# Horner's form for the numerator of a rational function: ScalarE makes one straight line in place of two, VectorE makes the rest

## The chip, the cores and the metric

The program runs on one core of a Trainium2 chip. The metric is the device time of one execution in microseconds (us); a median over several runs is given. The engines are named as in the profile: PE (TensorE, matmuls), PEld (its weight loads), DVE (VectorE), ACT (ScalarE), POOL (GpSimd) and SP (SyncE, which issues DMAs). SBUF is the on-chip memory of 128 partitions, PSUM the accumulator memory of 8 banks that PE writes.

## The reference

Two attentions (one over tokens averaged in fours, one over a band of 7 neighbours) are added, and the sum x of 4608 tokens by 512 goes through a two-layer network whose activation is a rational function:

```python
h = x @ w_in                                   # 4608 x 2048
h2 = h * h
h3 = h2 * h
P = a[0] + a[1] * h + a[2] * h2 + a[3] * h3
Q = 1.0 + np.abs(b[0]) * np.abs(h) + np.abs(b[1]) * h2
g = P / (Q + 1e-06)
return (g @ w_out).astype(np.float32)          # 4608 x 512
```

All is float32. The products with w_in and w_out are made with each operand split into a high and a low part, and three of the four part products are kept.

## The kernel before

The tokens are cut into ten blocks, eight of 512 tokens and two of 256 that collect remainders. A block of 512 tokens has 16 steps, one for each 128 columns of w_in; a block of 256 has 8 steps of 256 columns. That makes 144 steps, n = 0 to 143, and each handles a tile of 128 x 512 values of h.

A step has three parts. h_part makes h in one PSUM bank: 12 matmuls of 128x512 (L733), or in the first 16 steps 4 matmuls on unsplit operands (L721). The banks alternate: step n+2 writes the bank of step n, so it must wait until everything that reads h of step n has read it. middle (L748) turns h into g, as a high part gh and a low part gl. o_part, two steps later, multiplies gh and gl with the split w_out in 12 matmuls (L798) into four other banks that hold the block's output.

In middle, ScalarE reads h from PSUM four times: Abs with scale b0 into tb, Square into tq, and two straight lines, ta = a3*h + a2 and u = a1*h + a0 (all L746). VectorE then works on SBUF alone: tb = b1*tq + tb (L761), ta = ta*tq (L766), ta = ta + u (L767). ScalarE makes tq = exp(-ln(tb + 1.000001)), which is 1/Q, in two operations (Ln, Exp). VectorE makes gh = ta*tq (L770) and the low part by three more operations (L773, L778, L779). The tile u lies in the same memory as gh, and log (the result of Ln) in that of gl, so both can be written only when the o_part of step n-2 has read gh and gl.

The attention for a later block runs in between, in groups of two head pairs, called quads here. A quad is, for each pair: scores on PE (L417, L427), a maximum on DVE (L459, L466), exponentials on ACT (L474); pooled scores on PE (L444), their maximum on DVE (L489, L494), exponentials on ACT (L500); normalisation on DVE and ACT (L511, L512, L535, L517); transposes on PE (L548, L555) and copies of them on ACT (L561, L571, L572); and two groups of matmuls with v (L594, L582). The attention uses the PSUM banks 0 and 1. Two quads serve a block. The quads of the first block run ahead of step 0, those of the second in the first 16 steps, and twelve more between step 16 and step 112. In the first 16 steps the weights are also prepared (L338 to L361 on ACT and DVE).

The order on each engine is fixed before the program runs. A planner takes every piece of work with a cost in us, an engine and the tiles that it reads and writes, and places the pieces in a list (Plan.run); the engines then take their instructions strictly in that order. The planner knows of writes before reads and reads before writes. It holds no rule on two engines that read one tile. The framework under it adds the semaphore waits.

Of the kernel before, what the change touches and what calls it, by code (L numbers as in the profile page):

```python
# [13 lines left out]
AF = mybir.ActivationFunctionType  # L14
ALU = mybir.AluOpType
# [61 lines left out]
class Plan:  # L77
# [11 lines left out]
    def add(self, engine, dur, fn, reads=(), writes=(), due=None, lag=None):  # L89
        t = Task()  # L90
        t.engine, t.dur, t.fn, t.due, t.n = engine, dur, fn, due, len(self.tasks)
        t.lag, t.preds, t.succs, t.late, t.start = lag, {}, [], 1e9, None
        rk = set().union(*(r.keys for r in reads)) if reads else set()
        wk = set().union(*(w.keys for w in writes)) if writes else set()
        for k in rk | wk:
            w = self.writer.get(k)
            if w is not None:
                t.preds[w] = True
        for k in wk:
            for r in self.readers.get(k, ()):  # L100
                t.preds.setdefault(r, False)
            self.writer[k] = t
            self.readers[k] = []
        for k in rk - wk:
            self.readers[k].append(t) if k in self.readers else self.readers.__setitem__(k, [t])
        t.preds.pop(t, None)
        for p in t.preds:
            p.succs.append(t)
        self.tasks.append(t)
        return t  # L110
# [75 lines left out]
def attention_moe(  # L186
# [13 lines left out]
    scale = 1.0 / 8.0  # L200
    nc.scalar.preload_act_table_set("natural_log_exp_and_others")
    plan = Plan()
    add = plan.add
# [5 lines left out]
    def put(name, shape, dtype, at=None):  # L209
        nonlocal top  # L210
        offset = top if at is None else at
        n = 2 if dtype == BF16 else 4
        for d in shape[1:]:
            n *= d
        if at is None:
            top = -(-(offset + n) // 32) * 32
        ap = nc.alloc_sbuf_tensor_at(name, shape, dtype, offset=offset).ap()
        room = Room(ap, (("S", k) for k in range(offset // 32, -(-(offset + n) // 32))))
        room.at = offset
        room.size = n  # L220
        return room
# [26 lines left out]
    gb = [put(f"gb{i}", [P, DM], F32, g.at) for i, g in enumerate(gt)]  # L248
# [3 lines left out]
    cf = put("cf", [P, 8], F32)  # L252
# [47 lines left out]
    a0, a1, a2, a3 = (cf.ap[:, i : i + 1] for i in range(4))  # L300
# [405 lines left out]
    def bank_h(n):  # L706
        return banks[HFIRST[n]] if n < len(HFIRST) else hb[n % 2]
# [37 lines left out]
    def act(cost, out_, room_in, in_, func, *more, **kw):  # L745
        add("ACT", cost, lambda: nc.scalar.activation(out=out_.ap, in_=in_, func=func, **kw), (room_in, cf, *more), (out_,))  # L746

    def middle(n):  # L748

        ta, tb, tq = (mt[2 * i + n % 2] for i in range(3))  # L750
        gh, gl = gt[n % 2], gt[2 + n % 2]
        u, log = gb[n % 2], gb[2 + n % 2]
        h = bank_h(n)
        act(0.58, tb, h, h.ap, AF.Abs, scale=b0)
        act(0.48, tq, h, h.ap, AF.Square)
        act(0.66, ta, h, h.ap, AF.Identity, scale=a3, bias=a2)
        act(0.66, u, h, h.ap, AF.Identity, scale=a1, bias=a0)
        v = nc.vector
        add(
            "DVE", 0.66,  # L760
            lambda: v.scalar_tensor_tensor(  # L761
                out=tb.ap, in0=tq.ap, scalar=b1, in1=tb.ap, op0=ALU.mult, op1=ALU.add
            ),
            (tq, tb, cf), (tb,),
        )
        add("DVE", 0.61, lambda: v.tensor_tensor(out=ta.ap, in0=ta.ap, in1=tq.ap, op=ALU.mult), (ta, tq), (ta,))  # L766
        add("DVE", 0.61, lambda: v.tensor_tensor(out=ta.ap, in0=ta.ap, in1=u.ap, op=ALU.add), (ta, u), (ta,))  # L767
        act(0.63, log, tb, tb.ap, AF.Ln, bias=cone)
        act(0.54, tq, log, log.ap, AF.Exp, scale=-1.0)
        add("DVE", 0.61, lambda: v.tensor_tensor(out=gh.ap, in0=ta.ap, in1=tq.ap, op=ALU.mult), (ta, tq), (gh,))  # L770
        add(
            "DVE", 0.61,
            lambda: v.scalar_tensor_tensor(  # L773
                out=tb.ap, in0=tb.ap, scalar=CONE, in1=gh.ap.bitcast(F32), op0=ALU.add, op1=ALU.mult
            ),
            (tb, gh), (tb,),
        )
        add("DVE", 0.61, lambda: v.tensor_tensor(out=tb.ap, in0=ta.ap, in1=tb.ap, op=ALU.subtract), (ta, tb), (tb,))  # L778
        add("DVE", 0.61, lambda: v.tensor_tensor(out=gl.ap, in0=tb.ap, in1=tq.ap, op=ALU.mult), (tb, tq), (gl,))  # L779

    def o_part(n, f):
# [123 lines left out]
    for n in range(NS + LAG):  # L905
        if n < NS:
            k, s = steps[n]
            for f in range(blocks[k].fg):
                h_part(n, f)
                if n < NAT:  # L910
                    parts(0, n, due_h(n + blocks[0].nstep) - 2.0)
                    if n == NAT - 1 and NAT < blocks[0].nstep:
                        split_x(0, due_h(NAT) - 3.0)
            if s == blocks[k].nstep - 1:

                if k + 1 < len(blocks):
                    split_x(k + 1)
        o = n - LAG
        if o >= 0:
            k, s = steps[o]  # L920
            for f in range(blocks[k].fg):
                o_part(o, f)
            if s == blocks[k].nstep - 1:
                store(k)

                if blocks[k].b is None and blocks[k - 1].b + 2 < B:
                    attend(blocks[k - 1].b + 2)
                elif blocks[k].b is not None and blocks[k].b + 2 < B and blocks[k + 1].b is not None:
                    attend(blocks[k].b + 2)
        if n < NS:  # L930
            middle(n)
# [10 lines left out]
    for t in pe:  # L942
        n = int(WARM * (t.start - end) / 0.107)
# [91 lines left out]
```

## Time and profile before

| | us |
|---|---|
| median of 3 runs | 974.91 (974.35 to 976.29) |
| the profiled execution | 975.71 |
| its span in the trace | 973.9 |

The span is the time from the first to the last instruction of the program in the trace; the 1.8 us beside it lie around the span. The granted TensorE clock was 0.997 over the run.

The profile's page gives the busy time of each engine, a chain of work that ended last (followed back from the end, at each step to what released an instruction), and groups of instructions by line with their mean duration. Durations overlap a little: an engine starts its next instruction before the one ahead is quite finished, so the distance from start to start is shorter than the duration. A duration counts where another engine waits for the result, the distance where the engine itself is full.

| engine | busy, us | share of the span |
|---|---|---|
| PE | 959.7 | 99% |
| DVE | 838.4 | 86% |
| ACT | 810.5 | 83% |
| POOL | 147.1 | 15% |

### The profile page before, as it was taken

To read this page: it belongs to the slowest core of one execution; us is meant where nothing else is said; L and a number is where in the kernel's file an instruction comes from. 1 tells how busy PE (TensorE), PEld (TensorE's weight loads), DVE (VectorE), ACT (ScalarE), POOL (GpSimd) and SP (SyncE) were. 2 spreads that over 40 slices of the span, in tenths; PEclk is the share of its full clock that TensorE was granted. 3 is DMA by queue.
4 is the path that set the end of the run, shared out by engine and by line. 5 is a ranking of instruction groups with operands and counts; after the bars stand their busy time and mean duration, and the time that the engine had idled before them with its cause. 6 is when DMAs were issued, how large, how long until landed. Compare 5 with 4: busy or idle time off the path is not lost.

```text
span 973.9 us, 19825 instructions
## 1 busy us (share of the span) xinstructions
PE 959.7 (99%) x7383; PEld 759.8 (78%) x7383; DVE 838.4 (86%) x1474; ACT 810.5 (83%) x2076; POOL 147.1 (15%) x176
## 2 busy tenths in 40 slices
PE   7999999999999999999999999999999999999997
PEld 5665657887887879988878888878788787998885
DVE  6899999998888888888789887888788888888886
ACT  6899998978789887689787979798888988867774
POOL 1221322120302121002221121203030210000000
PEclk9999999999999999999999999999999999999999
DMA  9984654332424342023333333324243320100001
GB/s 318 297 264 126 160 126 114 76 69 69 83 94 65 87 73 73 1 60 68 76 76 94 85 66 86 85 85 86 66 83 100 56 46 2 44 1 23 1 1 43
DMA packets 46359, 83.43 MB, mean 86 GB/s; under 512 B 6552, under 2 KB 29080, under 8 KB 46264
## 3 DMA queue, kind: packets, MB, share of 16 engines
q1 hardware_dynamic: 25912, 63.00, 19.4%
q0 software_dynamic: 20352, 19.19, 14.3%
q8 instruction: 58, 0.95, 0.4%
q14 instruction: 37, 0.30, 0.1%
HBM read 72.72 MB, written 9.44 MB: 84 GB/s over the span
## 4 chain that ended last, share of the span: by engine, by line
PE 92%; ACT 5%; DVE 2%; issue 1%; DMA 0%; DVEq 0%; ACTq 0%
PE psum L798 40%; PE psum L733 37%; PE psum L721 4%; PE psum L582 3%; PE psum L594 2%; PE psum L548 2%; PE psum L555 2%; PE psum L427 2%; ACT el L474 2%; PE psum L444 1%; ACT m L746 1%; PE psum L417 1%; ACT ep L500 1%; PE psum L937 0%; ACT gb L746 0%
## 5 line engine op out<-in xcount | busy, mean ns | idle before, releaser
L798 PE MATMUL psum<-wh,g 128*128 128x512 f32 x1152 | 371.6, 404 | 0.9 <-DVE g L779 0.9
L733 PE MATMUL psum<-xs,wh 128*128 128x512 f32 (+1 forms) x1152 | 267.4, 369 | 0.0
L746 ACT ACTIVATE m<-psum,cf 128x512 f32<-128x512 f32 x288 | 215.9, 753 | 42.8 <-PE psum L733 40.6
L798 PEld LDWEIGHTS psum<-wh,g 128*128 128x128 f32 x1152 | 209.0, 189 | 49.4 <-issue 4.3
L733 PEld LDWEIGHTS psum<-xs,wh 128*128 128x128 f32 x1152 | 200.3, 189 | 36.9 <-ACT gb L746 0.3
L798 PE MATMUL psum<-wl,g 128*128 128x512 f32 x576 | 225.3, 392 | 0.0
L746 ACT ACTIVATE gb<-psum,cf 128x512 f32<-128x512 f32 x144 | 115.9, 805 | 48.4 <-PE psum L798 48.2
L394 POOL DMA_DIRECT2D pq<-in_qkp_dram x84 | 73.8, 908 | 468.5 <-DMA pq<-in_qkp_dram 384.1
L733 PE MATMUL psum<-xs,wl 128*128 128x512 f32 (+1 forms) x576 | 143.3, 371 | 0.0
L770 DVE TENSOR_TENSOR g<-m,m 128x512 fp32r<-128x512 f32 x144 | 99.2, 689 | 33.7 <-ACT m L746 31.6
L798 PEld LDWEIGHTS psum<-wl,g 128*128 128x128 f32 x576 | 108.6, 189 | 23.7
L767 DVE TENSOR_TENSOR m<-m,gb 128x512 f32<-128x512 f32 x144 | 99.2, 689 | 27.0 <-ACT gb L746 24.3
L761 DVE SCALAR_TENSOR_TENSOR m<-m,cf,m 128x512 f32<-128x512 f32 x144 | 107.4, 745 | 12.1 <-ACT m L746 11.9
L474 ACT ACTIVATE el<-psum,nm 128x64 f32<-128x64 f32 x320 | 97.5, 356 | 23.8 <-DVE nm L466 23.8
L733 PEld LDWEIGHTS psum<-xs,wl 128*128 128x128 f32 x576 | 100.0, 189 | 17.6 <-issue 1.0
L746 ACT ACTIVATE gb<-m,cf 128x512 f32<-128x512 f32 x144 | 107.2, 744 | 2.1 <-DVE m L761 2.1
L766 DVE TENSOR_TENSOR m<-m,m 128x512 f32<-128x512 f32 x144 | 98.5, 684 | 5.6 <-ACT m L746 5.6
L773 DVE SCALAR_TENSOR_TENSOR m<-m,g 128x512 f32<-128x512 f32 x144 | 99.4, 691 | 3.2
L778 DVE TENSOR_TENSOR m<-m,m 128x512 f32<-128x512 f32 x144 | 99.3, 690 | 2.7
L779 DVE TENSOR_TENSOR g<-m,m 128x512 fp32r<-128x512 f32 x144 | 98.2, 682 | 1.2
L746 ACT ACTIVATE m<-gb 128x512 f32<-128x512 f32 x144 | 93.3, 648 | 4.9 <-DVE m L766 2.1
L394 POOL DMA_DIRECT2D vp<-in_vp_dram x84 | 71.2, 880 | 164.1 <-DMA vp<-in_vp_dram 155.9
(64 smaller groups left out, 989.0 us busy)
## 6 DMA issues: line engine op xcount, KB each, us to landing
qk<-in_qk_dram SPq DMA_DIRECT2D x32, 590.0 KB
pq<-in_qkp_dram POOLq DMA_DIRECT2D x84, 144.0 KB, 3.3
vw<-in_vw_dram SPq DMA_DIRECT2D x32, 320.0 KB
out_dram<-xf SPq DMA_DIRECT2D x32, 256.0 KB
vp<-in_vp_dram POOLq DMA_DIRECT2D x84, 72.0 KB, 2.8
sx<-in_w_in_dram SPq DMA_DIRECT2D x11, 512.0 KB
sx<-in_w_out_dram SPq DMA_DIRECT2D x11, 512.0 KB
pq<-in_qkp_dram SPq DMA_DIRECT2D x28, 144.0 KB
```

Source lines behind the costliest of these rows:

```text
L394: lambda d=dst, x=src, r=r: nc.gpsimd.dma_start(out=d.ap, in_=x[b, r, :, i], accum_op=ALU.add),
L474: nc.scalar.activation(out=s.el.ap[:, k, c.pos(j), :], in_=view[:, j, k, :], func=AF.Exp, bias=nm[:, 5 * j + k : 5 * j + k + 1], scale=sca ...
L733: nc.tensor.matmul(ph.ap[:, f * t : (f + 1) * t], lhsT=(high, low)[j][0][fc].ap[:, c, :], rhs=blk.x[i].ap[:, c, :], start=(part_ == 0 and ...
L746: add("ACT", cost, lambda: nc.scalar.activation(out=out_.ap, in_=in_, func=func, **kw), (room_in, cf, *more), (out_,))
L761: lambda: v.scalar_tensor_tensor(out=tb.ap, in0=tq.ap, scalar=b1, in1=tb.ap, op0=ALU.mult, op1=ALU.add),
L766: add("DVE", 0.61, lambda: v.tensor_tensor(out=ta.ap, in0=ta.ap, in1=tq.ap, op=ALU.mult), (ta, tq), (ta,))
L767: add("DVE", 0.61, lambda: v.tensor_tensor(out=ta.ap, in0=ta.ap, in1=u.ap, op=ALU.add), (ta, u), (ta,))
L770: add("DVE", 0.61, lambda: v.tensor_tensor(out=gh.ap, in0=ta.ap, in1=tq.ap, op=ALU.mult), (ta, tq), (gh,))
L773: lambda: v.scalar_tensor_tensor(out=tb.ap, in0=tb.ap, scalar=CONE, in1=gh.ap.bitcast(F32), op0=ALU.add, op1=ALU.mult),
L778: add("DVE", 0.61, lambda: v.tensor_tensor(out=tb.ap, in0=ta.ap, in1=tb.ap, op=ALU.subtract), (ta, tb), (tb,))
L779: add("DVE", 0.61, lambda: v.tensor_tensor(out=gl.ap, in0=tb.ap, in1=tq.ap, op=ALU.mult), (tb, tq), (gl,))
L798: nc.tensor.matmul(ob[sub].ap, lhsT=g[i].ap[:, f0 : f0 + P], rhs=flat((high, low)[j][1][fc].ap), start=(fc == 0 and m == 0), stop=(fc == N ...
```

## The change

The numerator is computed in Horner's form without its constant: ta = a3*h + a2 on ScalarE as before, then ta = ta*h and ta = (ta + a1)*h on VectorE. The constant a0 is added inside the two later operations that use ta. The tile u and its ScalarE operation are gone. VectorE still has seven operations in a step. Two of them now read h from PSUM (L765 and L768 of the changed kernel), and three that took two tiles, or a tile and a constant of the instruction, take a constant per partition from cf as well.

```diff
-        u, log = gb[n % 2], gb[2 + n % 2]
+        log = gb[2 + n % 2]
...
         act(0.66, ta, h, h.ap, AF.Identity, scale=a3, bias=a2)
-        act(0.66, u, h, h.ap, AF.Identity, scale=a1, bias=a0)
...
-        add("DVE", 0.61, lambda: v.tensor_tensor(out=ta.ap, in0=ta.ap, in1=tq.ap, op=ALU.mult), (ta, tq), (ta,))
-        add("DVE", 0.61, lambda: v.tensor_tensor(out=ta.ap, in0=ta.ap, in1=u.ap, op=ALU.add), (ta, u), (ta,))
+        add("DVE", 0.66, lambda: v.tensor_tensor(out=ta.ap, in0=ta.ap, in1=h.ap, op=ALU.mult), (ta, h), (ta,))
+        add(
+            "DVE", 0.69,
+            lambda: v.scalar_tensor_tensor(out=ta.ap, in0=ta.ap, scalar=a1, in1=h.ap, op0=ALU.add, op1=ALU.mult),
+            (ta, h, cf), (ta,),
+        )
         act(0.63, log, tb, tb.ap, AF.Ln, bias=cone)
         act(0.54, tq, log, log.ap, AF.Exp, scale=-1.0)
-        add("DVE", 0.61, lambda: v.tensor_tensor(out=gh.ap, in0=ta.ap, in1=tq.ap, op=ALU.mult), (ta, tq), (gh,))
+        add(
+            "DVE", 0.66,
+            lambda: v.scalar_tensor_tensor(out=gh.ap, in0=ta.ap, scalar=a0, in1=tq.ap, op0=ALU.add, op1=ALU.mult),
+            (ta, tq, cf), (gh,),
+        )
...
-        add("DVE", 0.61, lambda: v.tensor_tensor(out=tb.ap, in0=ta.ap, in1=tb.ap, op=ALU.subtract), (ta, tb), (tb,))
+        add(
+            "DVE", 0.66,
+            lambda: v.scalar_tensor_tensor(out=tb.ap, in0=ta.ap, scalar=a0, in1=tb.ap, op0=ALU.add, op1=ALU.subtract),
+            (ta, tb, cf), (tb,),
+        )
```

The line numbers of the changed kernel are 12 higher after this place, up to 8 in the middle of it: L761, L766, L767, L770, L773, L778, L779, L798 of before are L760, L765, L768, L776, L781, L788, L791, L810 now; lines up to L746 keep their numbers.

The planner works from the changed list, so the order moves on every engine, and the framework's waits with it. The rows below are those of the built programs; "waits" names the engines (or DMA queues) whose semaphores an instruction waits for itself, and x4 four equal instructions.

**ACT in the quad at steps 99 and 100** (m0, m2, m4 are ta, tb, tq of an even step, m1, m3, m5 those of an odd one; el and ep belong to attention). Before, from the Square of step 99 on:

```order
L746 ACTIVATE m5_169<-psum 128x512
L746 ACTIVATE m1_165<-psum,cf_181 128x512
L474 ACTIVATE el1_203,sm1_188<-psum,nm1_184 128x64 [waits DVE_49,PE_49]
L474 ACTIVATE el1_203,sm1_188<-psum,nm1_184 128x64 x4
L746 ACTIVATE gb1_175<-psum,cf_181 128x512 [waits PE_49]
L474 ACTIVATE el1_203,sm1_188<-psum,nm1_184 128x64 x5
L746 ACTIVATE gb3_177<-m3_167,cf_181 128x512 [waits DVE_49]
L746 ACTIVATE m2_166<-psum,cf_181 128x512 [waits DVE_49,PE_49]
L746 ACTIVATE m5_169<-gb3_177 128x512 [waits Activation_49]
L746 ACTIVATE m4_168<-psum 128x512
L746 ACTIVATE m0_164<-psum,cf_181 128x512
L500 ACTIVATE ep0_199,sm0_187<-psum,nm0_183 128x144 [waits DVE_49,PE_49]
```

With the change, from the line ta of step 99 on:

```order
L746 ACTIVATE m1_165<-psum,cf_181 128x512 [waits PE_49]
L746 ACTIVATE m3_167<-psum,cf_181 128x512
L746 ACTIVATE m5_169<-psum 128x512 [waits DVE_49]
L474 ACTIVATE el1_203,sm1_188<-psum,nm1_184 128x64 [waits DVE_49,PE_49]
L474 ACTIVATE el1_203,sm1_188<-psum,nm1_184 128x64 x4
L746 ACTIVATE gb3_177<-m3_167,cf_181 128x512 [waits DVE_49,PE_49]
L474 ACTIVATE el1_203,sm1_188<-psum,nm1_184 128x64 x5
L746 ACTIVATE m5_169<-gb3_177 128x512 [waits Activation_49]
L746 ACTIVATE m0_164<-psum,cf_181 128x512 [waits PE_49]
L746 ACTIVATE m2_166<-psum,cf_181 128x512 [waits DVE_49]
L746 ACTIVATE m4_168<-psum 128x512 [waits DVE_49]
L500 ACTIVATE ep0_199,sm0_187<-psum,nm0_183 128x144 [waits DVE_49,PE_49]
```

The line ta now stands ahead of Abs and Square in a step, u is gone, and Square waits for DVE. Before, no Square of the 144 steps waited for DVE; now 73 do.

**DVE at the same place.** Before, from the last operation of step 98:

```order
L779 TENSOR_TENSOR g2_172<-m2_166,m4_168 128x512 [waits DVE_49]
L767 TENSOR_TENSOR m1_165<-m1_165,gb1_175 128x512 [waits DVE_49,Activation_49]
L489 TENSOR_REDUCE nm0_183<-psum 128x3 [waits PE_49]
L489 TENSOR_REDUCE nm1_184<-psum 128x3 [waits PE_49,Activation_49]
L494 TENSOR_TENSOR nm0_183<-nm0_183,scales_182 128x3 [waits DVE_49]
L494 TENSOR_TENSOR nm1_184<-nm1_184,scales_182 128x3 [waits DVE_49]
L770 TENSOR_TENSOR g1_171<-m1_165,m5_169 128x512 [waits Activation_49]
L761 SCALAR_TENSOR_TENSOR m2_166<-m4_168,cf_181,m2_166 128x512 [waits Activation_49]
L773 SCALAR_TENSOR_TENSOR m3_167<-m3_167,g1_171 128x512 [waits DVE_49]
L511 TENSOR_SCALAR sm0_187<-sm0_187 128x13 [waits Activation_49]
```

With the change, from the same operation:

```order
L791 TENSOR_TENSOR g2_172<-m2_166,m4_168 128x512 [waits DVE_49]
L768 SCALAR_TENSOR_TENSOR m1_165<-m1_165,cf_181,psum 128x512
L776 SCALAR_TENSOR_TENSOR g1_171<-m1_165,cf_181,m5_169 128x512 [waits DVE_49,PE_49,Activation_49]
L765 TENSOR_TENSOR m0_164<-m0_164,psum 128x512 [waits PE_49,Activation_49]
L489 TENSOR_REDUCE nm0_183<-psum 128x3 [waits PE_49]
L489 TENSOR_REDUCE nm1_184<-psum 128x3 [waits PE_49]
L494 TENSOR_TENSOR nm0_183<-nm0_183,scales_182 128x3 [waits DVE_49]
L494 TENSOR_TENSOR nm1_184<-nm1_184,scales_182 128x3 [waits DVE_49]
L781 SCALAR_TENSOR_TENSOR m3_167<-m3_167,g1_171 128x512
L760 SCALAR_TENSOR_TENSOR m2_166<-m4_168,cf_181,m2_166 128x512 [waits Activation_49]
```

gh of step 99 and L765 of step 100 now stand ahead of the pooled maxima. In the built program the count for which L765 of step 100 waits is that of Abs of the same step, the latest reader of its bank on ACT in the list, and not that of the line ta, whose result it uses; the Square behind waits for that L765. The accesses of ACT and DVE to one bank thus take turns, in the order of the list. The sequence in a step is ta, Abs, L765, Square, L768 in 63 of the 144 steps; ta, Abs, Square, L765, L768 in 32; ta, L765, L768, Abs, Square in 22; Abs, Square, ta, L765, L768 in 14; other mixtures in 13.

**PE behind the pooled scores of the same quad** (wh0 and wl0 are parts of w_in, wh1 and wl1 of w_out; g0 and g2 belong to step 98, g1 and g3 to step 99). Before, from the last o_part of step 98 on:

```order
L798 MATMUL psum<-wl1_10_140,g0_170 128x512
L733 MATMUL psum<-xs1_1_157,wh0_13_69 128x512 x4
L733 MATMUL psum<-xs1_0_156,wl0_13_114 128x512 x4
L733 MATMUL psum<-xs1_0_156,wh0_14_70 128x512 [waits Activation_49]
L733 MATMUL psum<-xs1_0_156,wh0_14_70 128x512 x3
L548 MATMUL psum<-ident_178,ep0_199 72x112 [waits Activation_49] x3
L548 MATMUL psum<-ident_178,ep0_199 72x112 [waits DVE_49]
L548 MATMUL psum<-ident_178,ep0_199 72x112 x2
L798 MATMUL psum<-wh1_11_83,g1_171 128x512 [waits DVE_49]
L798 MATMUL psum<-wh1_11_83,g3_173 128x512 [waits DVE_49]
```

With the change:

```order
L810 MATMUL psum<-wl1_10_140,g0_170 128x512
L733 MATMUL psum<-xs1_0_156,wh0_13_69 128x512 [waits DVE_49]
L733 MATMUL psum<-xs1_0_156,wh0_13_69 128x512 x3
L733 MATMUL psum<-xs1_1_157,wh0_13_69 128x512 x4
L733 MATMUL psum<-xs1_0_156,wl0_13_114 128x512 x4
L810 MATMUL psum<-wh1_11_83,g1_171 128x512 [waits DVE_49]
L810 MATMUL psum<-wh1_11_83,g3_173 128x512 [waits DVE_49]
```

The o_part of step 99 (wh1_11) comes straight behind h of step 101 (wh0_13); before, four matmuls of step 102 (wh0_14) and six transposes stood ahead of it. The first matmul into a bank waits for DVE where it waited for ACT. From step 24 on the list of PE switches to attention 110 times, where it did so 120 times.

## The prediction

> **What bounds the kernel now.** I read the page's busy times and chain first, then the chain in two stretches, then the windows.
>
> ```profile
> PE 959.7 (99%) x7383; PEld 759.8 (78%) x7383; DVE 838.4 (86%) x1474; ACT 810.5 (83%) x2076; POOL 147.1 (15%) x176
> PE 92%; ACT 5%; DVE 2%; issue 1%; DMA 0%; DVEq 0%; ACTq 0%
> by line: PE psum L798 43.1%; PE psum L733 43.0%; PE psum L582 2.8%; PE psum L427 2.2%; PE psum L548 2.2%; PE psum L594 2.2%; PE psum L555 2.1%; PE psum L444 1.7%; PE psum L417 1.0%
> ```
>
> The third line is the chain between 618 and 723 us, a whole block with its two quads: PE alone. Nothing that ACT or DVE gives up there shortens the run; only a new wait of PE counts. The chain leaves PE at the start, in one stretch of the first block, and at the end.
>
> ```profile
> 112.86 1.84 ACT m L746 x3
> ...
> 126.79 0.42 DVE wb L341
> ...
> 153.59 1.39 PE psum L582 x64
> 154.97 4.53 PE psum L798 x12
> 44.00:154.00 110.00, 107.71 (x720) 66.24 (x717) 107.80 (x205) 106.82 (x277) 24.24 (x29) 1.00 0.61 162
> 900.00:930.00 30.00, 30.00 (x134) 24.87 (x133) 25.95 (x40) 21.24 (x34) 0.00 (x0) 1.00 0.00 1
> 690.00:713.00 23.00, 23.00 (x171) 18.48 (x170) 17.40 (x34) 22.81 (x82) 4.38 (x5) 1.00 0.34 76
> ```
>
> The first four rows are pieces of the chain (start, length): from 112.86 to 153.59 us it alternates between ACT and DVE. The other three are windows (length, then busy PE, PEld, DVE, ACT, POOL, clock, DMA). From 44 to 154 us all three engines are nearly full. In a stretch without attention (900 to 930) DVE and ACT have room. In a quad (690 to 713) ACT is full, 22.81 of 23, and DVE idles because it waits for ACT and PE.
>
> **The change part by part.**
>
> ```profile
> L746 ACT ACTIVATE gb<-psum,cf 128x512 f32<-128x512 f32 x144 | 115.9, 805 | 48.4 <-PE psum L798 48.2
> L761 DVE SCALAR_TENSOR_TENSOR m<-m,cf,m 128x512 f32<-128x512 f32 x144 | 107.4, 745 | 12.1 <-ACT m L746 11.9
> L767 DVE TENSOR_TENSOR m<-m,gb 128x512 f32<-128x512 f32 x144 | 99.2, 689 | 27.0 <-ACT gb L746 24.3
> L773 DVE SCALAR_TENSOR_TENSOR m<-m,g 128x512 f32<-128x512 f32 x144 | 99.4, 691 | 3.2
> L535 DVE TENSOR_TENSOR el<-el,sm 128x640 f32<-128x640 f32 x32 | 26.2, 818 | 0.1
> L623 DVE TENSOR_TENSOR xf<-psum,up 128x464 f32<-128x464 f32 x32 | 19.2, 636 | 5.5 <-PE psum L582 5.3
> ```
>
> Removed: u, 144 x 0.805 = 115.9 us of ACT, and 48.2 us in which ACT stood at u until the o_part had read gh. Behind PE's chain this is worth nothing by itself. Log, in the memory of gl, still waits for that o_part.
>
> DVE keeps seven operations. Three become of the kind of L761 (745 ns, a constant per partition from cf) where they were of that of L767 (689 ns); an immediate constant costs nothing more (L773, 691). That is 3 x 0.056 = 0.17 us a step, 24 us in all. Reading PSUM has no price here: from 512 elements (L767) to 640 (L535) is 129 ns, 1.0 ns an element, so 464 elements would take 641 ns from SBUF, and L623 takes 636 with one input in PSUM. I take 0 for it. [...]
>
> In stretches without attention, 25.95 of 30 us of DVE grow by 0.9: 5.5 steps (30 over 2.72 + 2.74, the 12 matmuls of h and of o_part in rows below) x 0.17. PE hides that.
>
> *The turns at the bank.* This decides. Before, ACT alone read h. Now DVE reads it too, and the list of waits shows that L765 waits for Abs or Square, and Square or Abs for L765 or L768. The planner did not place its pieces for that. I walk the quad of steps 97 to 102 with starts and distances of the trace.
>
> ```profile
> 690.70 2.72 PE psum L733 x12
> 697.24 3.64 PE psum L733 x16
> 700.87 0.90 PE psum L444 x24
> 701.77 2.94 PE psum L798 x12
> 693.50 0.78 ACT L746 ACTIVATE gb<-m,cf 128x512 f32<-128x512 f32 x1
> 696.71 0.31 ACT L474 ACTIVATE el<-psum,nm 128x64 f32<-128x64 f32 x1 [0.18 <-DVE nm L466]
> 700.28 0.77 ACT L746 ACTIVATE gb<-m,cf 128x512 f32<-128x512 f32 x1
> 700.89 0.74 ACT L746 ACTIVATE m<-psum,cf 128x512 f32<-128x512 f32 x1
> 701.46 0.69 ACT L746 ACTIVATE m<-gb 128x512 f32<-128x512 f32 x1
> 702.46 0.85 ACT L746 ACTIVATE m<-psum,cf 128x512 f32<-128x512 f32 x1
> 703.12 0.45 ACT L500 ACTIVATE ep<-psum,nm 128x144 f32<-128x144 f32 x1
> 695.11 0.82 DVE L459 TENSOR_REDUCE nm<-psum 128x10 f32<-128x640 f32 x1 [2.20 <-PE psum L427]
> 701.80 1.12 DVE L489 TENSOR_REDUCE nm<-psum 128x3 f32<-128x432 f32 x2 [1.47 <-PE psum L444]
> 703.64 0.75 DVE L761 SCALAR_TENSOR_TENSOR m<-m,cf,m 128x512 f32<-128x512 f32 x1
> 704.30 0.69 DVE L773 SCALAR_TENSOR_TENSOR m<-m,g 128x512 f32<-128x512 f32 x1
> 706.79 0.63 DVE L779 TENSOR_TENSOR g<-m,m 128x512 fp32r<-128x512 f32 x1
> ```
>
> Distances: 0.66 us for L761's kind on DVE, 0.60 for the others; on ACT 0.61 (Ln), 0.57 (Abs), 0.5 (Exp), 0.66 (a line). A waiting engine starts some 0.07 us after the end of what it waits for.
>
> First turn. h of step 99 ends at 690.70 + 2.72 = 693.42. ACT ends the exponentials at 693.44 (0.06 sooner than Ln's 693.50, for Ln takes u's place among them), then Exp, the line ta of step 99 at 693.96, Abs at 694.62, which ends at 695.36. L765 of step 99 waits for that Abs: 695.43. The maximum L459 stands behind it and starts at 696.03 instead of 695.11, and so do the exponentials, 0.92 late: 697.63. Second turn. Two batches of them (1.46 and 1.44), Ln (0.61) and Exp (0.52) bring the line ta of step 100 to 701.66 and Abs to 702.32, end 703.06. L765 of step 100 waits for it, 703.13, and the pooled maxima L489 stand behind that: 703.73 instead of 701.80, 1.93 late. Behind them come their scaling, to 704.97, then L781, L760, L788, a small one and L791, which makes gl of step 99: 0.60 + 0.66 + 0.66 + 0.12 puts its start at 707.01 and its end 0.68 later at 707.69 (706.79 was the start before).
>
> PE without a wait: h of step 100 ends at 697.24 + 2.72 = 699.96; six matmuls of o_part (1.37), the pooled scores (0.90), six more (1.37), 12 of h (2.73) make 706.33. There the o_part of step 99 needs that gl, at about 707.75. PE stands for **1.4 us**. Before, four matmuls and six transposes lay there. Without the turns the same walk has L765 half a us sooner twice, and PE would wait 0.4. ACT and DVE stay late by as much for the rest of the quad, so I do not count it twice or take it back.
>
> The other kind of quad, around step 92, has L765 and L768 both ahead of Abs. There ACT had a gap, which takes up part:
>
> ```profile
> 640.87 0.31 ACT L474 ACTIVATE el<-psum,nm 128x64 f32<-128x64 f32 x1 [1.55 <-DVE nm L466]
> ```
>
> Its price lies between 0 and the 1.4 of the first kind; I take 0.8. Twelve quads lie behind step 16, six of each kind: 6 x 1.4 + 6 x 0.8 = **+13.2 us**. The ends are 0 (all hidden, below) and 12 x 1.4 = 16.8. [...]
>
> *First block.* DVE's idle time from 44 to 154 us is 110 - 107.80 = 2.2; 15 steps add 15 x 0.17 = 2.5 us. ACT loses 15 x 0.8 = 12 us there. DVE full, the stretch grows by 0.3 at least, and by 2.5 if the idle time stays. I take **+1.4**. Below nothing: rival two.
>
> *Switches of PE.* Twelve matmuls of L798 next to attention took 2.94 (above, 701.77), alone 2.74 (below). Ten switches fewer at 0.1 to 0.2: **-1.3**.
>
> *The end.*
>
> ```profile
> 959.69 2.74 PE psum L798 x12
> 962.45 1.40 ACT gb L746 x2
> 963.87 0.64 ACT m L746
> 964.53 0.70 DVE g L770
> 967.55 0.71 PE psum L798 x2
> ```
>
> At 962.45 u waits for the o_part of step 141, and Ln runs behind it. Now Ln starts there, 0.68 sooner, and gives 0.06 back in each of two VectorE operations: **-0.55**.
>
> Sum: 13.2 + 1.4 - 1.3 - 0.55 = +12.75 us. The profiled execution took 975.71, its span 973.9, so 988.5 by it. The median of the runs is 0.8 lower: **987.6 us**, 1.3% slower.
>
> **The rivals.**
>
> One, the turns are hidden. For it speaks that ACT has 4 x 0.8 = 3.2 us less in the four steps of a quad, more than 1.4. Against it, in the walk ACT idles for DVE, so it is late for order, not for load. Then +1.4 - 1.3 - 0.55 leaves 974.5 us, no change.
>
> Two, faster: the turns are hidden and the first block shrinks, ACT being its limit. Point of decision: whether DVE work not yet due (halves of w_in, 0.69 us each) moves behind 154 us, more than the 2.5 added. The ceiling is PE's idle time, 110 - 107.71 = 2.3, and 4.53 - 2.74 = 1.8 in the o_part at 154.97, together 4.1. Time 974.9 - 4.1 - 1.3 - 0.55 = 969 us. Against it stands DVE's 107.80 of 110.
>
> Three, worse: both kinds of quad cost 1.4 and the first block the full 2.5, with no gain from switches: 974.9 + 16.8 + 2.5 - 0.55 = 993.7 us; with PSUM reads that cost DVE more, a few more.
>
> **How the numbers follow.** Forecast 0.69, rival one 0.13, two 0.11, three 0.07. A measurement of this kernel can tell about 0.2%, 2 us, from no change. Slower by more: 0.69 + 0.07 = 0.76; within: 0.12, most of rival one; faster: 0.12, rival two and a rest of one. The range leaves out rival two and the far end of three, and takes in rival one: 973 to 996 us.
>
> **What would show it.** In the trace of after, PE must wait for DVE at L810 (gl, written by L791) or for copies of ACT at the transposes in each quad, about 1 us together, in places where before the chain was PE alone. ACT must idle at Square or Abs with DVE L765 or L768 named. L765 should take about 690 ns, L768, L776 and L788 about 745. The stretch from 900 us must keep its 2.72 + 2.74 us a step, and the last o_part come about 0.5 us nearer to the last h. If PE waits for nothing in the quads, or waits at the first matmul of h for L768 above all, my reason is wrong even if the time is right.

## The result and the profile after

| | before | after |
|---|---|---|
| median, us | 975.04 (974.35 to 976.29, 4 runs) | 1018.0 (1017.66 to 1019.75, 4 runs) |
| the profiled execution / its span, us | 975.71 / 973.9 | 1018.03 / 1015.1 |

The ratio is 1.0442, with a 95% interval of 1.0429 to 1.0454: 43 us slower, where 12.7 were forecast, and outside the range. The granted clock was 0.999, so none of it is the clock.

The page of after, busy times and the chain that ended last:

```profile
PE 978.2 (96%) x7383; PEld 759.0 (75%) x7383; DVE 867.5 (85%) x1474; ACT 725.8 (72%) x1932; POOL 147.2 (15%) x176
DVE 32%; PE 32%; ACT 30%; issue 4%; DMA 1%; ACTq 0%; DVEq 0%
```

No engine is full, and the chain, which was PE for 92%, now runs through DVE, PE and ACT by about a third each. Engines that wait for each other in a ring show here as falling shares (PE from 99 to 96%, DVE from 86 to 85%, ACT from 83 to 72%) in a span that grew from 973.9 to 1015.1 us. ACT gave up 85 us and nothing was won by it.

The groups of after (line, engine, operation, count; busy time and mean duration; idle time just before):

```profile
L765 DVE TENSOR_TENSOR m<-m,psum 128x512 f32<-128x512 f32 x144 | 98.3, 683 | 19.4 <-ACT m L746 18.3
L768 DVE SCALAR_TENSOR_TENSOR m<-m,cf,psum 128x512 f32<-128x512 f32 x144 | 106.6, 740 | 4.8 <-ACT m L746 3.9
L776 DVE SCALAR_TENSOR_TENSOR g<-m,cf,m 128x512 fp32r<-128x512 f32 x144 | 108.0, 750 | 73.2 <-ACT m L746 71.9
L810 PE MATMUL psum<-wh,g 128*128 128x512 f32 x1152 | 374.4, 403 | 11.0 <-DVE g L791 9.1
```

The operations themselves cost what was forecast: 683 ns with h from PSUM, 740 to 750 with a constant per partition. The loss is in waits. The list of waits of after (who waits, for what: us in total, times, longest):

```profile
ACT gb L746 <- DVE m L760: 97.2, 77, 2.7
DVE g L776 <- ACT m L746: 71.9, 88, 2.4
ACT m L746 <- DVE m L765: 58.6, 65, 1.7
DVE m L765 <- ACT m L746: 18.3, 44, 0.8
ACT m L746 <- DVE m L768: 11.9, 18, 1.2
```

The third and the fifth row are Square and Abs waiting for L765 and L768, the fourth is L765 waiting for ACT: the turns at the bank. The first two are the same delay seen further on, Ln waiting for tb and gh for Exp.

Where the time went is read from the starts of h on PE: the start of the first matmul of h of a step in a run, less that of before, and how this difference grows over a stretch. "First kind" are the six quads in steps 24 to 32, 40 to 48 and so on, "other kind" those in 16 to 24, 32 to 40 and so on; "without attention" is 48 to 56 and 120 to 143; "start" is everything up to step 16, "end" what lies behind the start of the last h. Some attention matmuls moved from a quad of the first kind to one of the other kind, so single kinds are compared between runs of one list, not with before.

| us of span, against before | start | first kind, six | other kind, six | without attention | end | sum |
|---|---|---|---|---|---|---|
| after | 2.9 | 7.1 | 25.2 | 3.9 | 2.0 | 41.1 |
| VectorE off the bank | 0.6 | -6.3 | 11.6 | 0.0 | 2.0 | 7.9 |
| the same, immediate constants | 0.8 | -6.8 | 10.8 | 0.0 | -0.8 | 4.1 |
| Square off the bank | 1.6 | 4.9 | 18.8 | 0.8 | 2.0 | 28.1 |
| Abs off the bank | 0.3 | -4.1 | 20.3 | 2.2 | 2.1 | 20.9 |

The four lower rows are experiments, told next. They keep every instruction of after in its place.

One thing disturbs the comparison with before. Its trace holds a stretch of 3.4 us in which the granted clock was half (0.50 in this window):

```profile
155.10:158.50 3.40, 3.40 (x9) 2.62 (x9) 3.12 (x6) 3.37 (x7) 1.26 (x2) 0.50 0.85 178
```

Matmuls of 128x512 start 0.43 us apart there, where 0.23 is usual, and the o_part at 154.97 took 4.53 us for 2.74. That is 1.8 us just ahead of step 16. After and the first two experiments of the table have no such stretch, so against an undisturbed before their start and their sum would be up to 1.8 us larger (an estimate from these two durations). Square off the bank and Abs off the bank have one each in steps 16 to 24; it costs some 1.6 us (an estimate: 8 matmuls 0.43 us apart take the place of 15 that are 0.23 apart) and belongs to neither wait.

### The profile page after: what moved, and what is told of

Read it like the earlier page. It is cut to its first block, busy times and chain, and to the rows that moved or that the text cites. A ratio compares the mean times of both kernels' runs of the same rounds, so it can differ in the third digit from the quotient of the medians.

```text
span 1015.1 us, 19663 instructions
## 1 busy us (share of the span) xinstructions
PE 978.2 (96%) x7383; PEld 759.0 (75%) x7383; DVE 867.5 (85%) x1474; ACT 725.8 (72%) x1932; POOL 147.2 (15%) x176
## 3 DMA queue, kind: packets, MB, share of 16 engines
q1 hardware_dynamic: 25912, 63.00, 18.8%
## 4 chain that ended last, share of the span: by engine, by line
DVE 32%; PE 32%; ACT 30%; issue 4%; DMA 1%; ACTq 0%; DVEq 0%
ACT m L746 13%; PE psum L733 12%; PE psum L810 11%; ACT el L474 7%; DVE m L765 5%; ACT gb L746 5%; DVE m L760 5%; DVE g L776 4%; DVE m L781 4%; DVE m L788 3%; DVE g L791 3%; DVE m L768 3%; PE psum L582 2%; ACT ep L500 2%; PE psum L594 2%
## 5 line engine op out<-in xcount | busy, mean ns | idle before, releaser
L810 PE MATMUL psum<-wh,g 128*128 128x512 f32 x1152 | 374.4, 403 | 11.0 <-DVE g L791 9.1
L733 PE MATMUL psum<-xs,wh 128*128 128x512 f32 (+1 forms) x1152 | 263.6, 369 | 3.1 <-ACT ep L500 3.1
L810 PEld LDWEIGHTS psum<-wh,g 128*128 128x128 f32 x1152 | 209.5, 188 | 69.6 <-DVE g L791 11.8
L746 ACT ACTIVATE m<-psum,cf 128x512 f32<-128x512 f32 x288 | 201.0, 735 | 37.8 <-PE psum L733 26.8
L810 PE MATMUL psum<-wl,g 128*128 128x512 f32 x576 | 224.8, 391 | 0.0
L746 ACT ACTIVATE gb<-m,cf 128x512 f32<-128x512 f32 x144 | 104.9, 728 | 117.2 <-DVE m L760 97.2
L776 DVE SCALAR_TENSOR_TENSOR g<-m,cf,m 128x512 fp32r<-128x512 f32 x144 | 108.0, 750 | 73.2 <-ACT m L746 71.9
L746 ACT ACTIVATE m<-psum 128x512 f32<-128x512 f32 x144 | 86.2, 599 | 65.7 <-DVE m L765 57.9
L810 PEld LDWEIGHTS psum<-wl,g 128*128 128x128 f32 x576 | 108.1, 188 | 22.8
L760 DVE SCALAR_TENSOR_TENSOR m<-m,cf,m 128x512 f32<-128x512 f32 x144 | 107.7, 748 | 17.5 <-ACT m L746 14.8
L765 DVE TENSOR_TENSOR m<-m,psum 128x512 f32<-128x512 f32 x144 | 98.3, 683 | 19.4 <-ACT m L746 18.3
L768 DVE SCALAR_TENSOR_TENSOR m<-m,cf,psum 128x512 f32<-128x512 f32 x144 | 106.6, 740 | 4.8 <-ACT m L746 3.9
L788 DVE SCALAR_TENSOR_TENSOR m<-m,cf,m 128x512 f32<-128x512 f32 x144 | 107.9, 749 | 2.6
L781 DVE SCALAR_TENSOR_TENSOR m<-m,g 128x512 f32<-128x512 f32 x144 | 99.2, 689 | 3.1
L791 DVE TENSOR_TENSOR g<-m,m 128x512 fp32r<-128x512 f32 x144 | 98.8, 686 | 1.0
L746 ACT ACTIVATE m<-gb 128x512 f32<-128x512 f32 x144 | 91.8, 638 | 3.0
```

The costliest lines, as they stand in the source:

```text
L733: nc.tensor.matmul(ph.ap[:, f * t : (f + 1) * t], lhsT=(high, low)[j][0][fc].ap[:, c, :], rhs=blk.x[i].ap[:, c, :], start=(part_ == 0 and ...
L760: lambda: v.scalar_tensor_tensor(out=tb.ap, in0=tq.ap, scalar=b1, in1=tb.ap, op0=ALU.mult, op1=ALU.add),
L765: add("DVE", 0.66, lambda: v.tensor_tensor(out=ta.ap, in0=ta.ap, in1=h.ap, op=ALU.mult), (ta, h), (ta,))
L768: lambda: v.scalar_tensor_tensor(out=ta.ap, in0=ta.ap, scalar=a1, in1=h.ap, op0=ALU.add, op1=ALU.mult),
L776: lambda: v.scalar_tensor_tensor(out=gh.ap, in0=ta.ap, scalar=a0, in1=tq.ap, op0=ALU.add, op1=ALU.mult),
L781: lambda: v.scalar_tensor_tensor(out=tb.ap, in0=tb.ap, scalar=CONE, in1=gh.ap.bitcast(F32), op0=ALU.add, op1=ALU.mult),
```

## The experiments

Five experiments change operands of after and nothing else: the first two, the two with one reader at a time, and the one with immediate constants. In the others the lists of the engines change too. A constant tile in SBUF (ident, repeated four times to 512 columns) stands in for h where an operation is taken off the bank.

**VectorE off the bank.**

```diff
-v.tensor_tensor(out=ta.ap, in0=ta.ap, in1=h.ap, op=ALU.mult)
+v.tensor_tensor(out=four(ta), in0=four(ta), in1=flat4, op=ALU.mult)
-v.scalar_tensor_tensor(out=ta.ap, in0=ta.ap, scalar=a1, in1=h.ap, ...)
+v.scalar_tensor_tensor(out=four(ta), in0=four(ta), scalar=a1, in1=flat4, ...)
```

> The changed kernel with its exact order on every engine, but the two VectorE operations behind the line ta read the constant identity tile from SBUF (four times side by side) in place of h from PSUM, so the numerator is not the reference's. No VectorE read of the bank is left: no turns, no PSUM price, and the bank is free after ScalarE's last read. The dearer constants per partition and the planner's new order stay. Theory (the turns of ScalarE and VectorE at the bank cost the time): 974 to 980 us. Rival one (VectorE's 0.17 us a step, or the new order itself, costs it): 1010 to 1020 us.

Measured: 983.65 us (one run; before 975.46). 34 of the 43 us are gone, so the shared bank makes most of the loss; but 8 remain, more than the theory allowed. Its page has the chain back on PE for the greater part:

```profile
PE 962.4 (98%) x7383; PEld 757.5 (77%) x7383; DVE 861.3 (88%) x1474; ACT 720.3 (73%) x1932; POOL 146.8 (15%) x176
PE 56%; DVE 23%; ACT 16%; DMA 2%; issue 2%; SPq 1%; DVEq 0%; ACTq 0%
```

**ScalarE's Abs and Square off the bank**, VectorE still on it.

```diff
-act(0.58, tb, h, h.ap, AF.Abs, scale=b0)
-act(0.48, tq, h, h.ap, AF.Square)
+act(0.58, four(tb), h, flat4, AF.Abs, scale=b0)
+act(0.48, four(tq), h, flat4, AF.Square)
```

> The changed kernel with its exact order, but ScalarE's Abs and Square read the constant identity tile from SBUF in place of h, so the denominator is not the reference's. ScalarE reads the bank once, for the line ta, on which VectorE's first operation depends anyway; VectorE reads h from PSUM twice and holds the bank until the second one, as in the changed kernel. Theory (turns): 974 to 982 us. Rival two (the bank is held longer, until VectorE's second read, or VectorE's reads of PSUM are dear): 1005 to 1020 us.

Measured: 989.15 us (one run). Here VectorE reads h from PSUM twice in each step and holds the bank up to L768, and yet 29 us are gone, though the time lies outside both expectations. It loses 5.5 us of span more than the run before; by the same kind of table 2.8 of them lie at the start and 1.8 in steps 16 to 24, and from step 64 on no stretch differs by more than 0.2. The trace has a stretch of 3.4 us at half the clock in each of these two places (at 28.8 and 196.1 us; the clock over the run was 0.995), which explains the 1.8 and perhaps part of the 2.8. Reading PSUM from VectorE and holding the bank longer are thus not what costs most; the waits between the two readers are.

**The planner told of the turns** (the complete computation): a piece that reads a PSUM bank counts readers of that bank on other engines as predecessors.

```diff
         for k in rk:
+            if k[0] == "P":
+                for r in self.readers.get(k, ()):
+                    if r.engine != engine:
+                        t.preds.setdefault(r, False)
```

> The changed kernel, complete, but the planner is told that readers of one PSUM bank on two engines come one behind the other in the order in which the code names them: ScalarE's three reads first, then VectorE's two. The waits stay, but no ScalarE instruction waits for VectorE at the bank any more. Theory (turns that the planner does not know): 975 to 990 us, most of the 43 us gone. If the turns cost their time wherever they stand: over 1005 us.

Measured: 996.47 us (994.15 to 998.0, 4 runs; ratio 1.0214, 1.0196 to 1.0232). The sequence at the bank becomes ta, Abs, Square, L765, L768 in 129 steps, and no reader on ScalarE waits for VectorE at the bank any more, but only half the loss comes back: the time lies between the two expectations. The sharing itself stays, with its waits all on VectorE, and Ln now waits for VectorE's tb for 146.2 us in all. Whether another order hides the rest wasn't tried.

**h copied to SBUF** (the complete computation): ScalarE copies h into the place of u, and VectorE reads the copy.

```diff
+act(0.66, u, h, h.ap, AF.Identity)
-v.tensor_tensor(out=ta.ap, in0=ta.ap, in1=h.ap, op=ALU.mult)
+v.tensor_tensor(out=ta.ap, in0=ta.ap, in1=u.ap, op=ALU.mult)
```

(and u.ap for h.ap in the operation of L768.)

> The changed kernel, complete, but ScalarE copies h into the old place of u in SBUF, and VectorE's two operations read that copy. ScalarE has its fourth operation back, the planner makes a new order, VectorE keeps its three dearer operations. Theory (turns): 974 to 980 us, as before the change. Rival one (dearer VectorE operations): 990 us or more.

Measured: 978.29 us (977.3 to 979.51, 7 runs; ratio 1.0033, 1.0022 to 1.0045). With the same VectorE operations and a fourth ScalarE operation a step back, 40 of the 43 us are gone. Busy times and the group of the first product from its page:

```profile
PE 958.5 (98%) x7383; PEld 757.9 (78%) x7383; DVE 869.0 (89%) x1474; ACT 788.6 (81%) x2076; POOL 147.5 (15%) x176
...
L766 DVE TENSOR_TENSOR m<-m,gb 128x512 f32<-128x512 f32 x144 | 98.3, 683 | 23.2 <-ACT gb L746 22.8
```

It takes 683 ns from SBUF, the same as L765 from PSUM. With the copies ScalarE is busy for 63 us more (788.6 against 725.8), and that time lies beside PE's, as u's did.

**One reader at a time off the bank**, Square alone, then Abs alone (the edit of the second experiment, one line of it in each).

> The changed kernel with its exact order, but Square alone reads the constant identity tile in place of h, so the denominator is not the reference's. In the 63 steps with the sequence ta, Abs, L765, Square, L768, ScalarE no longer waits for VectorE at the bank; VectorE still waits for Abs. In the 22 steps with L765 and L768 ahead, Abs still waits. Loop theory (Square behind L765 ties the two engines into one serial loop of L765, Square, L760, Ln, Exp, L776, L781, L788 and the next L765, longer than PE's step): 988 to 1000 us, with the 2.8 us lost between the starts of steps 128 and 143 gone. Rival (it is VectorE's wait for Abs that delays, as the prediction walked it): 1008 us or more.

> The changed kernel with its exact order, but Abs alone reads the constant identity tile in place of h, so the denominator is not the reference's. VectorE's L765 now waits only for the line ta that it needs, but Square still waits for L765 in 63 steps and for L768 in 29 more. Loop theory: the loop has lost nothing but Abs's place, 1003 to 1016 us, the loss between steps 128 and 143 stays above 1 us. Rival (VectorE's wait for Abs): 988 to 1000 us.

Measured: 1004.46 and 996.56 us (one run each), 13.5 and 21.4 us less than after; together 35, about what both give in the first experiment. So the two waits nearly add up, and they rule different places. Without Abs on the bank the six quads of the first kind give back 11.2 of the 13.4 us that leaving the bank altogether gives back there; without Square only 2.2. In the stretches without attention it is the other way: Square 3.1 of 3.9, Abs 1.7. In the other kind of quad Square gives back 6.4 and Abs 4.8 of 13.6, and each some 1.6 more but for the half clock in steps 16 to 24. So Square's time lies between the two forecasts, and that of Abs is the rival's: a ring through Square rules the stretches without attention, but in the quads of the first kind it is VectorE's wait for Abs, as the prediction had walked it.

**Immediate constants**, on top of the first experiment.

```diff
-scalar=a1, in1=flat4
+scalar=0.5, in1=flat4
-scalar=a0, in1=tq.ap
+scalar=0.25, in1=tq.ap
-scalar=a0, in1=tb.ap
+scalar=0.25, in1=tb.ap
```

> As the run in which VectorE's two operations on h read a constant tile in place of h (983.7 us), in the same order of every instruction, but the three operations that took a constant per partition from cf in place of none or an immediate (two with a0, one with a1) take an immediate of 0.25 or 0.5. So neither the turns at the bank nor the dearer constants are left, and the numerator is not h's and has other constants. What remains over the kernel before is the order alone. Theory, order: the 8 us that were left come from the order of the pieces, so this takes 980 to 984 us, and the quads of the other kind still lose 1.5 to 2 us each. Rival, constants: 0.17 us a step on VectorE's chain in the quads made them, so this takes 974 to 979 us and the quads of the other kind lose under 0.7 us.

Measured: 979.83 us (979.79 to 980.35, 3 runs; ratio 1.0043, 1.002 to 1.0066), 0.2 us below what the order theory allowed and 0.8 above the rival's range, so nearer to the first. By spans (981.9 and 978.0) the 8 us that were left split evenly: 3.9 from the constants, 4.1 from the new order (up to 5.9 against a before without the half clock). The quads go as the order theory has them (the other kind still shows its 1.8 us each); the constants act elsewhere, 2.8 of their 3.9 us at the end. Two groups of this run:

```profile
L778 DVE SCALAR_TENSOR_TENSOR g<-m,m 128x512 fp32r<-128x512 f32 x144 | 99.3, 690 | 78.7 <-ACT m L746 76.8
L767 DVE TENSOR_TENSOR m<-m,ident 128x512 f32<-128x512 f32 x144 | 98.8, 686 | 6.6 <-ACT m L746 6.5
```

The operation that makes gh takes 690 ns with an immediate, 750 with a constant from cf (L776 of after).

**The planner told the old costs and reads, and the same off the bank.** It is told what it was told before the change, with an empty piece in place of u.

```diff
+add("ACT", 0.66, lambda: None, (h, cf), (u,))
-add("DVE", 0.66, ..., (ta, h), (ta,))
+add("DVE", 0.61, ..., (ta, tq), (ta,))
-    (ta, h, cf), (ta,),
+    (ta, u, h), (ta,),
```

> The complete changed computation, but the planner is told of the pieces as in the kernel before: their old costs, their old reads, and an empty piece in place of u, so the middle of a step stands in the lists nearly where it stood before (ta*h where ta*tq stood, behind tb's operation; the other where ta + u stood). In 15 to 20 places in a hundred the lists still differ from before in the neighbourhood. The turns at the bank remain: VectorE reads h behind what ScalarE did before it in the list. Theory, turns: the loss is made by two engines that read one bank and by VectorE holding it, in whatever order they were not planned for, so this takes 995 to 1020 us. Rival, new order: the loss comes from the new order, in which L765 stands ahead of Square and of tb's operation, so the old order brings it down to 975 to 988 us.

> The kernel that was planned as before (1018.8 us), instruction for instruction in the same order, but VectorE's two operations on h read a constant tile in SBUF in place of h, so the numerator is not h's and no VectorE operation reads the banks of h. Theory, turns: in that order too the loss is made by the shared bank, so this takes 974 to 984 us, as the same edit did with the order of the change (983.7). Rival, order: the loss in this order is one of the order itself (VectorE's products stand where they stood, but the tiles they need come in another sequence on ScalarE), so this takes over 1000 us.

Measured: 1018.82 us (1017.65 to 1019.98, 2 runs; ratio 1.0447, 1.0413 to 1.0481), and 1006.19 off the bank (one run). The lists that came out are not those of before, though. Counted as the longest sequence that two lists share, 1131 of 1515 instructions of ScalarE and 1074 of 1474 of VectorE stand as in before; in after it is 1203 and 1026, so these lists are no nearer to it. Whether the old order would bring the time back is thus not tested. But the second run takes the conclusion away that the turns alone are why: in this order they are worth 13.7 us of span, and 30.5 remain without them. Some 8 of the 30.5 are the clock (an estimate, 5 x 1.6), since this trace holds five stretches of 3.4 us at half of it, with 0.991 over the run (that of the run with the turns holds four, with 0.993); the rest is still more than the theory of the turns allowed. The rival comes nearer: an order that was planned with other reads and costs than the kernel's loses by itself. What loses in it isn't shown; ScalarE's longest wait for VectorE there is Ln's for tb, 137.3 us in all (97.2 in after). What the turns cost thus depends on the order around them; the 33 us hold for the order of the change.

**A version without VectorE on the bank and with one operation less** (the complete computation). With the line ta = a3*h + a2 and the square tq, (tq + a1/a3)*ta is a3*h^3 + a2*h^2 + a1*h and a constant, which the later operations subtract where they added a0. One VectorE operation replaces two, and it reads SBUF only. It needs a3 other than zero.

```diff
-add("DVE", 0.66, lambda: v.tensor_tensor(out=ta.ap, in0=ta.ap, in1=h.ap, op=ALU.mult), (ta, h), (ta,))
-v.scalar_tensor_tensor(out=ta.ap, in0=ta.ap, scalar=a1, in1=h.ap, op0=ALU.add, op1=ALU.mult)
+v.scalar_tensor_tensor(out=ta.ap, in0=tq.ap, scalar=a1, in1=ta.ap, op0=ALU.add, op1=ALU.mult)
```

(here a1 holds a1/a3, divided once at the start, and a0 the constant to subtract.)

> Complete. The second line of h is made from the first: a1*h + a0 = (a1/a3)*(a3*h + a2) + d, so VectorE computes ta = (tq + a1/a3)*ta in one operation and adds d where the change adds a0. It needs a3 other than zero. ScalarE has three reads of h and VectorE none, VectorE six operations a step in place of seven. No turns, no h held for VectorE, less work on both engines. By the theory PE is then the bound nearly everywhere: 968 to 975 us, the gain over the kernel before coming from the first block and the end. If some other property of the change (the missing fourth ScalarE operation, the dearer operations with a constant per partition) costs the time: over 978 us.

Measured: 971.35 us (970.95 to 972.77, 5 runs; before 974.94, 9 runs; ratio 0.9963, 0.9949 to 0.9976). It is faster than both kernels. Its page:

```profile
PE 957.6 (99%) x7383; PEld 759.4 (78%) x7383; DVE 782.4 (81%) x1333; ACT 724.6 (75%) x1932; POOL 146.7 (15%) x176
PE 93%; ACT 4%; DVE 2%; DMA 1%; issue 0%; DVEq 0%; ACTq 0%; SPq 0%
```

It saves 86 us of ScalarE and 56 of VectorE and gains under 4, since PE bounds it. By the starts of h 2.4 us of the gain lie up to step 16 and 0.8 at the end, but up to 1.8 of the 2.4 are the half clock in the trace of before. The medians are 3.6 us apart in runs of like clock (0.997 to 1.0 each), so the place of part of the gain is open.

## Why the prediction was wrong

The mechanism in the quads and the sign were right, the size was off by a factor of 3.4. The runs split the 41.1 us of span into turns at the bank, 33.2 (after less the first experiment); dearer constants, 3.9; the new order, 4.1 (up to 5.9, as said above). Three steps of the prediction failed: the turns in the quads were costed too low, "PE hides that" was wrong outside the quads, and the end was forecast as a saving where it is a loss.

**The turns in the quads: the terms 6 x 1.4 and 6 x 0.8, mis-sized.** Of the 1.4 the walk left 0.4 to stand without the turns, so its turns came to 6 x 1.0 + 6 x 0.8 = 10.8 us. They measured 13.4 + 13.6 = 27.0: 2.2 to 2.3 us a quad in each kind.

In the first kind the walk found the right place and the right wait. PE in after, in the quad that it walked (start, length, and in brackets the idle time and what ended it):

```profile
722.73 0.64 PE L417 MATMUL psum<-maskb,identb 64*64 64x320 bf16 x4
...
730.27 1.39 PE L444 MATMUL psum<-pq 64*64 64x144 f32 x24
...
737.08 0.50 PE L810 MATMUL psum<-wh,g 128*128 128x512 f32 x1 [0.86 <-DVE g L791]
```

The third row is the o_part of step 99 waiting for gl, as walked. The same three places with Abs off the bank (L812 is the o_part there):

```profile
708.35 0.33 PE L417 MATMUL psum<-maskb,identb 64*64 64x320 bf16 x4
...
715.58 0.97 PE L444 MATMUL psum<-pq 64*64 64x144 f32 x24
...
720.69 0.81 PE L812 MATMUL psum<-wh,g 128*128 128x512 f32 x2
```

No wait for gl is left. From h of step 101 to h of step 102 after takes 1.16 us longer than in the first experiment, with the same list of PE: that is the price of this wait, near the 1.0 of the walk. (The walk let a waiting engine start 0.07 us after the end of what it waits for; where L765 waits for ScalarE it is 0.03 in after, in 44 waits, which would take some 0.1 off the 1.0.) Where the walk went wrong is its "PE without a wait". The first two rows are score matmuls: 0.64 and 1.39 us where they took 0.33 and 0.97. The two steps in which they lie lost 0.29 and 0.45 against the first experiment, and the step behind the wait another 0.32; together 2.2. Scores go into the attention's banks, which ACT's exponentials must free, and the walk itself made those 0.92 us late without asking what PE would find there. (That PE waited for them at this place is argued, for the trace names no releaser; in the other kind, below, it names the exponentials.)

In the other kind the term was not walked; it was taken down from 1.4 because of a gap of 1.55 us in ACT "which takes up part". Rows of after at that quad:

```profile
663.52 0.69 DVE L765 TENSOR_TENSOR m<-m,psum 128x512 f32<-128x512 f32 x1 [0.25 <-ACT m L746]
...
666.71 0.82 DVE L459 TENSOR_REDUCE nm<-psum 128x10 f32<-128x640 f32 x1
...
668.36 0.31 ACT L474 ACTIVATE el<-psum,nm 128x64 f32<-128x64 f32 x1 [1.32 <-DVE nm L466]
...
672.14 0.33 PE L417 MATMUL psum<-maskb,identb 64*64 64x320 bf16 x3 [0.19 <-ACT el L474]
...
679.28 0.95 PE L444 MATMUL psum<-pq 64*64 64x144 f32 x20 [0.17 <-ACT el L474]
...
688.65 0.66 PE L555 MATMUL psum<-ident,el 128*128 128x128 f32 x4 [0.76 <-ACT ept L561]
```

The gap is still there, 1.32 us: ACT spends it waiting for the maximum L459, which stands on VectorE behind an L765 that itself waited for ACT. It is no slack but part of the same ring, and the exponentials come later by what VectorE is late. PE then waits three times behind ACT, and the steps from h of 92 to h of 95 lose 0.47, 0.62 and 1.06 us against the first experiment, 2.15 together. The waits with a releaser in these rows make 1.1 of that.

**Stretches without attention: "PE hides that", wrong.** The prediction compared busy time (25.95 of 30 us) with the added 0.17 a step. What counts is a ring: gh of a step, the operations behind it, L765 of the next step, then its Square, its tb (L760), Ln, Exp and its gh. VectorE and ACT in after, around step 124:

```profile
892.72 0.75 DVE L776 SCALAR_TENSOR_TENSOR g<-m,cf,m 128x512 fp32r<-128x512 f32 x1 [0.86 <-ACT m L746]
...
894.89 0.68 DVE L765 TENSOR_TENSOR m<-m,psum 128x512 f32<-128x512 f32 x1
...
895.61 0.60 ACT L746 ACTIVATE m<-psum 128x512 f32<-128x512 f32 x1 [1.68 <-DVE m L765]
...
896.24 0.75 DVE L760 SCALAR_TENSOR_TENSOR m<-m,cf,m 128x512 f32<-128x512 f32 x1
...
897.09 0.72 ACT L746 ACTIVATE gb<-m,cf 128x512 f32<-128x512 f32 x1 [0.88 <-DVE m L760]
...
898.51 0.75 DVE L776 SCALAR_TENSOR_TENSOR g<-m,cf,m 128x512 fp32r<-128x512 f32 x1 [0.86 <-ACT m L746]
```

From gh to gh it is 5.79 us, where PE needs 2.72 + 2.74 = 5.46 a step (5.62 in this block of 256 tokens, by the starts of h). With Square off the bank, and then with VectorE off the bank and immediates, gh follows gh in the same list and the same two steps:

```profile
881.32 0.75 DVE L778 SCALAR_TENSOR_TENSOR g<-m,cf,m 128x512 fp32r<-128x512 f32 x1 [0.86 <-ACT m L746]
...
886.96 0.75 DVE L778 SCALAR_TENSOR_TENSOR g<-m,cf,m 128x512 fp32r<-128x512 f32 x1 [0.86 <-ACT m L746]
```

```profile
859.69 0.69 DVE L778 SCALAR_TENSOR_TENSOR g<-m,m 128x512 fp32r<-128x512 f32 x1 [0.91 <-ACT m L746]
...
865.22 0.69 DVE L778 SCALAR_TENSOR_TENSOR g<-m,m 128x512 fp32r<-128x512 f32 x1 [0.92 <-ACT m L746]
```

5.64 and 5.53. So Square's wait adds 0.15 us to each turn of the ring and the two constants that lie in it 0.11. In the last steps of before, of 512 tokens, the ring held pace with PE's 5.44:

```profile
921.02 0.69 DVE L770 TENSOR_TENSOR g<-m,m 128x512 fp32r<-128x512 f32 x1 [0.58 <-ACT m L746]
...
926.45 0.69 DVE L770 TENSOR_TENSOR g<-m,m 128x512 fp32r<-128x512 f32 x1 [0.58 <-ACT m L746]
```

The distance from the start of h to that of gh, 7.7 us there, grows in after to 10.8 by step 130 and, once PE has waited, again to 10.9 by step 140; at about that point the o_part, which follows two steps (10.9 us) behind, has to wait. That cost 3.9 us where 0 was forecast.

**The end: -0.55 forecast, +2.0 measured.** The saving is real, but covered: with the immediates the end comes 0.8 earlier, and its chain is PE alone:

```profile
964.56 7.78 PE psum L812 x34
```

With the constants the ring reaches the last step 2.0 us later behind its h (9.7 from h to gh against 7.7), and the whole of it shows, since nothing follows that could take it up. The constants were costed by the work that lies beside them, but they stand in the ring.

**First block: +1.4 forecast, +2.9 measured** with the start; 0.6 off the bank. (Up to 4.7 and 2.4, if the half clock in before is taken out.) The window of after:

```profile
44.00:154.00 110.00, 106.49 (x689) 64.45 (x686) 105.61 (x195) 97.62 (x259) 24.21 (x28) 1.00 0.61 162
```

VectorE is idle for 4.4 us of the 110 where it was for 2.2: it did not get fuller, it waits. **The switches of PE, -1.3,** can't be told apart: the new order as a whole costs 4.1 or more, and this term lies in it.

**What held.** The reading of PSUM: 683 ns with h in PSUM, 683 and 686 with the tile in SBUF, so its price of 0 stands; the few us more that rival three adds for PSUM reads that cost VectorE more are shown by no run. The constant: 60 ns where 56 were taken. The waits: in the trace of after no read of a bank by ScalarE overlaps one by VectorE; the nearest two are 0.03 us apart. What an overlap would do isn't shown. In the order of the change these waits came to 33.2 us. Rival one (hidden) fell with its reason, ACT's lighter load: ACT is idle for order. Rival two was blind to the ring, and 1.8 of the 4.1 us that it counted as PE's idle time are the half clock. Rival three had the right side, but no term outside the quads and the first block.

## What to carry to other kernels

Before a second engine is made to read a PSUM bank, look for what it needs in SBUF already (here the square and the line), or let the first reader copy it: the copies took 63 us of ScalarE, and that kernel is within 3 us of before, dearer constants and all; the sharing cost 33 us. When instructions move between engines, follow the ring that leads from one step's result through the other engine into the next step's, and compare its length with the step of the bounding engine; the busy shares of before, 86% for VectorE and 83% for ScalarE, said nothing about it. And a gap on an engine is slack only if what ends it isn't late for the same reason, as it was for the 1.32 us in the other kind of quad.

## What the runs showed of the hardware

A constant per partition cost VectorE 60 ns on a tile of 128 x 512 in float32 (750 against 690 ns, the same operation with an immediate), while an input from PSUM cost nothing beside SBUF (683 against 683 and 686). Taking Square and Abs off the bank one by one gave back 13.5 and 21.4 us, and taking VectorE off 34.4, so the two waits nearly add up. In a stretch of 3.4 us with half the granted clock matmuls of 128x512 started 0.43 us apart in place of 0.23, and before had one of these stretches.
